# The weight conversion's stores begun by GpSimd instead of SyncE, and the post-softmax mix two places behind the pre-softmax mix

## The chip, the cores and the metric

One core of a Trainium2 chip. The metric is device time in microseconds (us) of one execution. Engines: PE (TensorE matmul; its weight loads are shown as PEld), DVE (VectorE), ACT (ScalarE), POOL (GpSimd), SP (SyncE, which here only begins DMAs).

## What is computed

Attention with heads mixed before and after the softmax, then a feed-forward layer. Cut to what matters:

```python
# batch 8, heads 12, seq 448, head_dim 64
scores = q @ k^T / 8                                   # per head
scores = einsum('bhij,hg->bgij', scores, w_pre)        # heads mixed
attn   = softmax over j
attn   = einsum('bhij,hg->bgij', attn, w_post)         # heads mixed again
x      = (attn @ v), rows = tokens (3584), columns = 12*64 = 768
h      = x @ w_in          # 768 x 2048, "in" weights
g      = h - tanh(h)
out    = g @ w_out         # 2048 x 768, "out" weights
```

## The kernel before, in words

The program has two stages. The first is attention (until about 845 us of the profile); the second is the feed-forward layer, whose products need each weight split into a rounded part and a remainder, and some sums and differences of weight quarters. This splitting, the **weight conversion**, is done during attention, on DVE, ACT and POOL, which have time left there.

**Attention.** Tokens of a batch come in blocks of 120 (the last has 88); a block's scores lie in SBUF as a tile `s`. Ten tokens by 12 heads make a group of 120 rows. A *place* handles two groups; there are 180 places (`NPL`), written out in Python in one loop over `p`, and every engine runs its instructions in exactly the order in which they are written (`in_order`). In place `p`:

1. SP begins the gathers `t<-s` (L907) of the groups that place `p+2` will need (`gather`, six tiles `t`), and then up to six waiting transfers of two lists, `queue` (loads of q, k, v and stores of x) and `slow` (the conversion's). A transfer is put in a list in one place and begun by SP in a later one (`issue`).
2. PE does the **premix** (`ps_p`, L918, 8 matmuls) of place `p`. Its two banks `ps_p` are the only ones, so it needs the exponents of place `p-1` to be finished.
3. `norm(p-1)`: DVE adds an epsilon to the sums and inverts them (`zs`, L938, L939), POOL multiplies them into the mixing weights (`wr`, L940).
4. `expo(p)`: DVE finds the row maxima (`mx`, L927, two), ACT the exponents (`e`, L929, two, four tiles).
5. PE does the jobs of the place: transposes of q and k (`ps_m` L840, L814), `scores` of a later block (`ps_q`, L874), and `values` (`ps_m`, L999), the product with v of an earlier block. The list `halved` gives each half of a block's scores ("s") and values ("v") an earliest and a latest place, and the loop behind it chooses.
6. PE does the **mix** of place `p-1` (`ps_o`, L957, 32 matmuls; one buffer of two banks), which needs `e` and `wr` of place `p-1`. ACT copies the result to `at` (L967, L974) at the start of the next place.

**The conversion.** `Convert.place` runs at the start of places 5 to 180. It takes a quad of four 128x128 weight pieces through the stages of the generator `narrow_quad`, one stage a place; 48 quads in all. Its DVE instructions (L81, L82, L90, L91, L94) stand ahead of the place's `zs` and `mx` in DVE's order, its POOL instructions (L84 to L131) ahead of the place's `wr`. Each quad is loaded as `cr` (two DMAs), and leaves by two stores of 512 KB, `co` and `ct`, to the tensors `wi`, `ss` (in) or `wo`, `ts` (out). The argument `dma` of `narrow_quad` puts these stores in the list `slow`, so SP begins them one place later or more.

POOL begins DMAs itself only in the feed-forward stage (`gs`, `go` and results, L647, L669, L670, L362, L519).

Of the kernel before, what the change touches and what calls it, by code (L numbers as in the profile page):

```python
# [10 lines left out]
F32 = mybir.dt.float32  # L11
# [10 lines left out]
def raw(ap):  # L22

    return ap.bitcast(F32)
# [10 lines left out]
class Convert:  # L35


    def __init__(self, nc, pool, dma, items, places):
        self.nc, self.pool, self.dma = nc, pool, dma
        self.todo, self.loads, self.active = list(items), [], []  # L40
        self.rate, self.due = len(self.todo) / places, 1.0

    def load(self):
# [6 lines left out]
    def place(self):  # L50
        for x in list(self.active):
            next(x[0], None)
            x[1] += 1
            if x[1] == 7:
                self.active.remove(x)
        self.due = min(self.due + self.rate, 1.3)
        if self.due >= 1.0 and len(self.active) < 2 and not [x for x in self.active if x[1] < 4] and self.loads and self.loads[0][1]():
            r, _, to = self.loads.pop(0)
            self.active.append([narrow_quad(self.nc, self.pool, self.dma, r, *to), 1])
            next(self.active[-1][0])  # L60
            self.due -= 1.0
        if self.todo and len(self.loads) < 2 and len(self.loads) + len([x for x in self.active if x[1] < 5]) < 3:
            self.load()

    def rest(self, between):
        while self.todo or self.loads or self.active:
            self.due = 1.0
            self.place()
            between()


def narrow_quad(nc, pool, dma, r, dst, sums, sums_dst):

    p = r.shape[0]
    hi, lo = r[:, :, :, 1], r[:, :, :, 0]
    u, w = hi, lo


    lim = 122879.9921875
    m = pool.tile([p, 4, 128], F32, name="cm", tag="cm", bufs=2)  # L80
    nc.vector.tensor_scalar(m, hi.bitcast(F32), lim, -lim, op0=ALU.min, op1=ALU.max)  # L81
    nc.vector.tensor_scalar(w, lo, 8, None, op0=ALU.logical_shift_right)  # L82
    yield
    nc.gpsimd.tensor_scalar(m, m, 2.0**-112, None, op0=ALU.mult)  # L84
    nc.scalar.mul(w.bitcast(F32), w, 2.0**-44)
    yield
    o = pool.tile([p, 4, 2, 128], F32R, name="co", tag="co", bufs=2)
    oh, ol = o[:, :, 0], o[:, :, 1]
    s = ol.bitcast(I32)
    nc.vector.tensor_scalar(s, hi, -(2**31), None, op0=ALU.bitwise_and)  # L90
    nc.vector.scalar_tensor_tensor(  # L91
        out=u, in0=m.bitcast(I32), scalar=3, in1=s, op0=ALU.logical_shift_left, op1=ALU.bitwise_or
    )
    nc.vector.tensor_scalar(s, u, -(2**23), None, op0=ALU.bitwise_and)  # L94
    yield
    nc.gpsimd.tensor_tensor(out=m, in0=w.bitcast(F32), in1=s.bitcast(F32), op=ALU.mult)
    nc.gpsimd.tensor_tensor(out=m, in0=m, in1=u.bitcast(F32), op=ALU.add)
    yield
    t = pool.tile([p, 4, 2, 128], F32, name="ct", tag="ct", bufs=2)
    nc.scalar.copy(oh, m)  # L100
    done = sums(nc, m, t[:, :, 1])
    yield
    nc.gpsimd.tensor_sub(ol, m, raw(oh))
    done()
    nc.gpsimd.tensor_copy(t[:, :, 0].bitcast(F32R), t[:, :, 1])
    dma(dst, raw(o).rearrange("p x t n -> p x (t n)"))
    yield
    nc.gpsimd.tensor_sub(t[:, :, 1].bitcast(F32R), t[:, :, 1], t[:, :, 0])
    dma(sums_dst, t.rearrange("p s t n -> p s (t n)"))


def sums_in(nc, m, t):
# [38 lines left out]
def kernel_body(  # L151
# [11 lines left out]
    nc = tc.nc  # L163
    B, H, S, D = q.shape
    P = 128
# [204 lines left out]
    class Results:  # L370
# [145 lines left out]
        def store(self, b, t, h, c):  # L516
            to = out[b * TB + t * TT : b * TB + (t + 1) * TT, h * N2 : (h + 1) * N2]
            eng = nc.gpsimd if self.n_gr < len(self.grs) else nc.sync
            eng.dma_start(to, c.rearrange("p c n -> p (c n)"))  # L519
# [216 lines left out]
    with ExitStack() as st:  # L736
# [184 lines left out]
        def expo(p, pss):  # L921
            zs = gp.tile([P, 3, 2], F32, name="zs", tag="zs")
            es = []
            for r, ps in enumerate(pss):

                mx = gp.tile([P, 1], F32, name="mx", tag="mx")
                nc.vector.tensor_reduce(out=mx, in_=ps, axis=AX.X, op=ALU.max, negate=True)  # L927
                e = gp.tile([P, S], F32, name="e", tag="e", bufs=4)
                nc.scalar.activation(e, ps, AF.Exp, bias=mx, scale=1.0, accum_out=zs[:, 0, r : r + 1])  # L929
                es.append(e)  # L930
            te[p] = [es, zs]
# [222 lines left out]
        for i in range(len(blocks)):  # L1154

            f0, f1, f2 = first[i : i + 3]
            if i + 1 < len(blocks):
                lo = max(0, (f0 - 1) // 2 - 1)
                hi = f1 // 2 - 3
                for x in range(0 if i else 1, 3):  # L1160
                    e = lo + 2 * x if lo + 4 <= hi else lo + (hi - lo) * x // 2
                    halved.append((e if i else x - 1, hi, "s", i + 1, x))
            for x in range(2):
                halved.append(((f1 - 1) // 2 + 2, f2 // 2 + 1 if f2 < NG else NPL + 7, "v", i, x))
        at_s, p, kind = {}, 0, None
        window = {i: (lo, hi) for lo, hi, k, i, _ in sorted(halved, reverse=True) if k == "s"}
        while halved:
# [84 lines left out]
            NPL - 1: [partial(load_w0, 1)],  # L1252
            NPL + 1: [block0.step],
        }
        mixed = None
        for p in range(NPL + 3):
            if mixed:
                mixed()
                mixed = None
            if 5 <= p < NPL + 1:  # L1260
                conv.place()
            place[0] += 1
            for t in (2 * p + 4, 2 * p + 5):
                if t < NG:
                    gather(t)
            issue(6)
            if p == NPL + 1:
                for f in start.pop(p):
                    f()
            if p < NPL:  # L1270
                ps = premix(p)
            if 1 <= p < NPL + 1:
                norm(p - 1)
            if p == NPL:
                for f in x0[1:]:
                    f()
            if p < NPL:
                expo(p, ps)
            if p > NPL:
                next(xq)  # L1280
                next(xq)
            for f, *a in todo[p]:
                f(*a)
            for f in sooner:
                f()
            sooner.clear()
            if 1 <= p < NPL + 1:
                mixed = mix(p - 1)
            for f in then + last:
                f()  # L1290
            then.clear()
            last.clear()
            if p == NPL - 3:
                conv.rest(now)
                early.close()
                open_early()
            if p == NPL - 1:
                early_ps.close()
                open_ps_h()
            for f in start.get(p, ()):  # L1300
                f()
            for _ in range(pieces.get(p, 0)):
                next(xl)
# [91 lines left out]
```

## Time and profile before

| | |
|---|---|
| three runs | 1707.81 us median (1704.64 to 1708.6) |
| the profiled execution | 1703.0 us, its span 1701.3 us |
| mean granted TensorE clock | 0.994 |
| busy in the span: PE, DVE, ACT, POOL | 1660.1, 1231.3, 1091.1, 585.5 us |
| DMAs begun by SP (queue q1) | 414.34 MB |
| DMAs begun by POOL (queue q0) | 57.68 MB |

The page lists, for each engine, how long it was busy; a view by stages gives the same for stretches of the span, with the granted clock of TensorE ("PEclk", 1.00 is full) and the busy share of the 16 DMA engines. "A <- B" in a list of waits means that A stood idle until B was done. In a timeline the columns are start, duration, engine, line and operation, and in brackets the idle time of that engine just before, with what ended it.

### The profile page before, as it was taken

How to read it: one execution, taken by the hardware profiler on the slowest of the kernel's cores; microseconds unless marked ns; L12 is line 12 of the kernel's file. 1: busy time of each engine (PE TensorE's matmuls, PEld its weight loads, DVE VectorE, ACT ScalarE, POOL GpSimd, SP SyncE). 2: the span in 40 equal slices, each digit the busy share in tenths (PEclk: the TensorE clock that was granted, in tenths of full speed). 3: DMA queues.
4: the chain of work that ended last, by engine and by line, in shares of the span. 5: the costliest groups of instructions: out<-in, count | busy, mean ns of one | idle time of the engine just before them, and what ended most of it. 6: DMA issues, size and time to landing. Idle time of an engine off the chain costs nothing.

```text
span 1701.3 us, 41215 instructions
## 1 busy us (share of the span) xinstructions
PE 1660.1 (98%) x16068; PEld 1379.8 (81%) x16068; DVE 1231.3 (72%) x2119; ACT 1091.1 (64%) x1920; POOL 585.5 (34%) x798
## 2 busy tenths in 40 slices
PE   8999999999999899999999999999999999999999
PEld 6777777777777677677788888888888888989999
DVE  5777777878777777675497899868778867778432
ACT  5777777777777677676586777556667456666331
POOL 1466667666666666662100111101001101011100
PEclk9999999999999999999999999999999999999999
DMA  8879889898987979856589899989999989988993
GB/s 183 218 228 257 255 246 276 247 270 259 256 253 231 269 234 257 254 182 208 190 269 340 273 331 318 346 295 335 318 334 362 368 272 327 326 311 327 404 413 132
DMA packets 322290, 475.09 MB, mean 279 GB/s; under 512 B 105264, under 2 KB 255280, under 8 KB 322096
## 3 DMA queue, kind: packets, MB, share of 16 engines
q1 hardware_dynamic: 305660, 414.34, 75.5%
q0 software_dynamic: 16128, 57.68, 8.7%
q8 instruction: 128, 2.10, 0.5%
q14 instruction: 66, 0.54, 0.1%
q10 hardware_dynamic: 308, 0.43, 0.1%
HBM read 274.73 MB, written 120.59 MB: 232 GB/s over the span
## 4 chain that ended last, share of the span: by engine, by line
PE 72%; DMA 7%; DVE 7%; ACT 4%; issue 4%; POOL 4%; SPq 1%; POOLq 0%; ACTq 0%; DVEq 0%
PE ps_o L957 11%; PE ps_h L291 8%; PE ps_h L292 7%; PE ps_h L294 7%; PE ps_m L999 6%; PE ps_p L918 6%; PE y L534 6%; PE y L532 6%; PE y L533 6%; PE ps_q L874 4%; DMA t<-s 2%; DMA gl<-gs 2%; ACT e L929 1%; DVE mx L927 1%; PE y L504 1%
## 5 line engine op out<-in xcount | busy, mean ns | idle before, releaser
L957 PEld LDWEIGHTS ps_o<-wr,e 60*112 60x112 f32 (+1 forms) x5760 | 303.3, 175 | 46.1 <-POOL wr L940 31.9
L957 PE MATMUL ps_o<-wr,e 60*112 60x60 f32 (+1 forms) x5760 | 314.5, 259 | 16.1 <-POOL wr L940 14.6
L929 ACT ACTIVATE e<-ps_p,mx 128x448 f32<-128x448 f32 x360 | 224.8, 631 | 117.2 <-DVE mx L927 82.8
L927 DVE TENSOR_REDUCE mx<-ps_p 128x1 f32<-128x448 f32 x360 | 206.5, 615 | 109.1 <-PE ps_p L918 108.5
L967 ACT COPY at<-ps_o 112x960 f32<-112x960 f32 x156 | 154.3, 989 | 103.4 <-PE ps_o L957 102.9
L918 PE MATMUL ps_p<-t,wpre 60*64 60x448 f32 (+1 forms) x1440 | 182.4, 570 | 6.7 <-DMA t<-s 6.6
L999 PEld LDWEIGHTS ps_m<-at,vr 112*64 112x64 f32 x3072 | 147.6, 137 | 23.0 <-issue 7.7
L999 PE MATMUL ps_m<-at,vr 112*64 112x120 f32 (+1 forms) x3072 | 161.4, 262 | 1.1 <-DMA vr<-in_v_dram 0.9
L532 PE MATMUL y<-w,gh 128*128 128x384 f32 x448 | 151.2, 338 | 2.1 <-DMA w<-wo 1.6
L940 POOL TENSOR_TENSOR wr<-wpost,zs 128x120 f32<-128x120 f32 x180 | 70.0, 389 | 237.6 <-DVE zs L939 199.0
L533 PE MATMUL y<-w,gh 128*128 128x384 f32 x448 | 150.5, 336 | 0.0
L534 PE MATMUL y<-w,gl 128*128 128x384 f32 x424 | 143.4, 338 | 3.0 <-DVE gl L450 3.0
L874 PEld LDWEIGHTS ps_q<-kk,qh 64*120 64x120 f32 (+1 forms) x768 | 59.1, 174 | 82.0 <-issue 45.1
L874 PE MATMUL ps_q<-kk,qh 64*120 64x448 f32 (+1 forms) x768 | 121.8, 394 | 0.9 <-ACT kk L825 0.4
L879 DVE COPY s<-ps_q 120x448 f32<-120x448 f32 (+1 forms) x192 | 112.2, 614 | 9.8 <-PE ps_q L874 8.0
L669 POOL DMA_DIRECT2D gs<-gb x24 | 17.2, 717 | 291.6 <-DVE gb L668 291.6
L307 ACT ACTIVATE u<-h 128x1024 f32<-128x1024 f32 x56 | 59.5, 1063 | 74.4 <-DVE h L716 70.5
L879 ACT COPY s<-ps_q 120x448 f32<-120x448 f32 (+1 forms) x192 | 94.9, 538 | 7.1 <-PE ps_q L874 6.7
L647 POOL DMA_DIRECT2D gs<-ga x24 | 17.2, 716 | 230.0 <-DVE ga L330 222.9
L532 PEld LDWEIGHTS y<-w,gh 128*128 128x128 f32 x448 | 84.2, 188 | 7.2 <-issue 3.5
L533 PEld LDWEIGHTS y<-w,gh 128*128 128x128 f32 x448 | 84.1, 188 | 3.4
L534 PEld LDWEIGHTS y<-w,gl 128*128 128x128 f32 x424 | 79.6, 188 | 4.6 <-DVE gl L450 4.6
(372 smaller groups left out, 3971.3 us busy)
## 6 DMA issues: line engine op xcount, KB each, us to landing
t<-s SPq DMA_DIRECT2D x342, 210.0 KB
wa<-ss SPq DMA_DIRECT2D x96, 384.0 KB
w<-wo SPq DMA_DIRECT2D x43, 768.0 KB
gl<-gs SPq DMA_DIRECT2D x62, 512.0 KB
wa<-wi SPq DMA_DIRECT2D x72, 384.0 KB
w<-ts SPq DMA_DIRECT2D x35, 768.0 KB
gs<-gs POOLq DMA_DIRECT2D x24, 768.0 KB, 9.2
cr<-in_moe_w_in_dram SPq DMA_DIRECT2D x48, 256.0 KB
```

The source lines that it names most:

```text
L291: nc.tensor.matmul(ph, w[:, c, 0], xh, start=start and c == 0, stop=False, skip_group_check=True)
L532: nc.tensor.matmul(y, gh[:, tok], wh, start=first, stop=False, skip_group_check=True)
L533: nc.tensor.matmul(y, gh[:, tok], wl, start=False, stop=False, skip_group_check=True)
L534: nc.tensor.matmul(y, gl[:, tok], wh, start=False, stop=last, skip_group_check=True)
L874: nc.tensor.matmul(ps[:n, :S], qx[a, hp, :], kx[a, hp % 2], start=(x == 0), stop=(x == 2))
L879: eng(sts[i][:n, 2 * hp + j, :], ps[:n, :S])
L918: nc.tensor.matmul(pss[r][halves[j], :], wpre[k, :], ts[j][k, :], start=True, stop=True)
L927: nc.vector.tensor_reduce(out=mx, in_=ps, axis=AX.X, op=ALU.max, negate=True)
L929: nc.scalar.activation(e, ps, AF.Exp, bias=mx, scale=1.0, accum_out=zs[:, 0, r : r + 1])
L957: nc.tensor.matmul(ps[:CP, j, c * GP : (c + 1) * GP].rearrange("p (h i) -> p h i", i=GI)[:, :, r * GH : (r + 1) * GH], e[k, c * CP : (c + ...
L967: nc.scalar.copy(ats[i0][:, :, :, at : at + 2 * GI].rearrange("p c h (j i) -> p j (c h) i", j=2), ps[:CP, :, : NC * GP].rearrange("p j (x ...
L999: nc.tensor.matmul(pv[j * D : (j + 1) * D, r, :n], vt[:, j, c, :], ats[i][:, c, 2 * hp + j, :n], start=(c == 0), stop=(c == NC - 1),)
```

## The change

Three things are edited. First, `narrow_quad` hands its stores to a list `done`, and a new method `Convert.stores`, called in each place just behind `norm(p-1)`, begins what is in it with `nc.gpsimd.dma_start`. Second, the mix of place `p-2` instead of `p-1` is written in place `p`, with the exponents in six tiles instead of four; in the last place (`NPL`) two mixes are left and are written one behind the other, with ACT's copy between them. The values of a block are allowed one place later. Third, the SBUF that is set aside for the DMAs that POOL begins is halved, 4096 to 2048 bytes.

```diff
-        self.todo, self.loads, self.active = list(items), [], []
+        self.todo, self.loads, self.active, self.done = list(items), [], [], []
...
-            self.active.append([narrow_quad(self.nc, self.pool, self.dma, r, *to), 1])
+            self.active.append([narrow_quad(self.nc, self.pool, lambda *x: self.done.append(x), r, *to), 1])
...
+    def stores(self):
+        for x in self.done:
+            self.nc.gpsimd.dma_start(*x)
+        self.done.clear()
...
-def narrow_quad(nc, pool, dma, r, dst, sums, sums_dst):
+def narrow_quad(nc, pool, store, r, dst, sums, sums_dst):
...
-    dma(dst, raw(o).rearrange("p x t n -> p x (t n)"))
+    store(dst, raw(o).rearrange("p x t n -> p x (t n)"))
...
-    dma(sums_dst, t.rearrange("p s t n -> p s (t n)"))
+    store(sums_dst, t.rearrange("p s t n -> p s (t n)"))
...
-                e = gp.tile([P, S], F32, name="e", tag="e", bufs=4)
+                e = gp.tile([P, S], F32, name="e", tag="e", bufs=6)
...
-                halved.append(((f1 - 1) // 2 + 2, f2 // 2 + 1 if f2 < NG else NPL + 7, "v", i, x))
+                halved.append(((f1 - 1) // 2 + 3, f2 // 2 + 2, "v", i, x) if f2 < NG else ((f1 - 1) // 2 + (3 if f1 < NG else 2), NPL + 7, "v", i, x))
...
         for p in range(NPL + 3):
-            if mixed:
-                mixed()
-                mixed = None
+            for f in mixed:
+                f()
+            mixed.clear()
...
             if 1 <= p < NPL + 1:
                 norm(p - 1)
+            conv.stores()
...
-            if 1 <= p < NPL + 1:
-                mixed = mix(p - 1)
+            if 2 <= p < NPL + 1:
+                mixed.append(mix(p - 2))
+            if p == NPL:
+                mixed.pop()()
+                mixed.append(mix(p - 1))
...
-    nc = _bacc.Bacc("TRN2", target_bir_lowering=False, num_devices=1, dynamic_dma_scratch_size=4096)
+    nc = _bacc.Bacc("TRN2", target_bir_lowering=False, num_devices=1, dynamic_dma_scratch_size=2048)
```

Line numbers behind the new method are 6 higher in the changed kernel (the mix is L963, the premix L924, `wr` L946, the values L1005).

How the order moves. On PE, from the premix of place 1 on, before:

```order
L918 MATMUL ps_p<-t,wpre 64x448 x4
L874 MATMUL ps_q<-kk,qh 120x448 x4
L874 MATMUL ps_q<-kk,ql 120x448 x2
L957 MATMUL ps_o<-wr,e 112x12x5 x16
L918 MATMUL ps_p<-t,wpre 64x448 x4
```

and with the change:

```order
L924 MATMUL ps_p<-t,wpre 64x448 x4
L880 MATMUL ps_q<-kk,qh 120x448 x4
L880 MATMUL ps_q<-kk,ql 120x448 x2
L924 MATMUL ps_p<-t,wpre 64x448 x4
L880 MATMUL ps_q<-kk,qh 120x448 x4
L880 MATMUL ps_q<-kk,ql 120x448 x2
L963 MATMUL ps_o<-wr,e 112x12x5 x16
```

Place 1 has no mix any more; the first mix stands behind the premix of place 2. (A row of the mix or the premix counts each matmul once, where the profile counts two passes.)

At the end of attention on PE, before (`ps_h` is the first product of the feed-forward layer):

```order
L957 MATMUL ps_o<-wr,e 112x12x5 x16
L918 MATMUL ps_p<-t,wpre 64x448 x4
L999 MATMUL ps_m<-at,vr 64x120 x24
L957 MATMUL ps_o<-wr,e 112x12x5 x16
L918 MATMUL ps_p<-t,wpre 64x448 x4
L957 MATMUL ps_o<-wr,e 112x12x5 x32
L291 MATMUL ps_h<-xh,w_13143 128x512
```

and with the change:

```order
L963 MATMUL ps_o<-wr,e 112x12x5 x16
L924 MATMUL ps_p<-t,wpre 64x448 x4
L1005 MATMUL ps_m<-at,vr 64x120 x24
L963 MATMUL ps_o<-wr,e 112x12x5 x16
L924 MATMUL ps_p<-t,wpre 64x448 x4
L1005 MATMUL ps_m<-at,vr 64x120 x24
L963 MATMUL ps_o<-wr,e 112x12x5 x48
L297 MATMUL ps_h<-xh,w_13097 128x512
```

Behind the last premix stood two mixes (x32); now a product of values and three mixes (x48) stand there.

On POOL, the second half of a quad's conversion, before:

```order
L940 TENSOR_TENSOR wr<-wpost,zs 128x2x60
L103 TENSOR_TENSOR co<-cm,co 128x4x128
L105 CAST ct<-ct 128x4x128
L940 TENSOR_TENSOR wr<-wpost,zs 128x2x60
L108 TENSOR_TENSOR ct<-ct 128x4x128
L96 TENSOR_TENSOR cm<-cr,co 128x512
L97 TENSOR_TENSOR cm<-cm,cr 128x512
L940 TENSOR_TENSOR wr<-wpost,zs 128x2x60
```

and with the change:

```order
L946 TENSOR_TENSOR wr<-wpost,zs 128x2x60
L109 TENSOR_TENSOR co<-cm,co 128x4x128
L111 CAST ct<-ct 128x4x128
L946 TENSOR_TENSOR wr<-wpost,zs 128x2x60
L67 DMA wi_65<-co 512x1x256
L114 TENSOR_TENSOR ct<-ct 128x4x128
L102 TENSOR_TENSOR cm<-cr,co 128x512
L103 TENSOR_TENSOR cm<-cm,cr 128x512
L946 TENSOR_TENSOR wr<-wpost,zs 128x2x60
L67 DMA ss_77<-ct 512x1x256
```

Each store stands just behind a `wr`; 96 such DMAs are on POOL, and SP's order has 96 fewer.

More of the change, by code (lines that the diff above doesn't have):

```diff
@@ L68, in rest @@
             self.place()
+            self.stores()
             between()
-def narrow_quad(nc, pool, dma, r, dst, sums, sums_dst):
+def narrow_quad(nc, pool, store, r, dst, sums, sums_dst):
     p = r.shape[0]
@@ L1254, in kernel_body @@
         }
-        mixed = None
+        mixed = []
         for p in range(NPL + 3):
-            if mixed:
-                mixed()
-                mixed = None
+            for f in mixed:
+                f()
+            mixed.clear()
             if 5 <= p < NPL + 1:
```

## Prediction

> **What bounds the kernel now.** I read the page's busy times first, then the stages, then what PE waited for in attention.
>
> ```profile
> PE 1660.1 (98%) x16068; PEld 1379.8 (81%) x16068; DVE 1231.3 (72%) x2119; ACT 1091.1 (64%) x1920; POOL 585.5 (34%) x798
> ```
>
> ```profile
> core 0: us, PE busy (x) PEld busy (x) DVE busy (x) ACT busy (x) POOL busy (x), PEclk, DMA share, GB/s
> 60.00:760.00 700.00, 680.61 (x9930) 521.58 (x9925) 523.69 (x1315) 500.82 (x1146) 470.53 (x597) 0.99 0.83 248
> 760.00:870.00 110.00, 107.38 (x1434) 84.19 (x1431) 63.49 (x146) 70.67 (x146) 20.80 (x37) 0.98 0.65 211
> 870.00:1701.00 831.00, 817.16 (x4116) 732.74 (x4114) 610.51 (x576) 484.84 (x553) 82.85 (x128) 1.00 0.89 321
> ```
>
> PE is the bound in every stage. In the 700 us in which the conversion runs, PE is idle for only 19.4 us, and POOL for 229.5. The change adds or removes no work on PE, so all that it can win is PE's idle time in attention, some 20 us, and what the clock loses there. The feed-forward stage I take as it is: what POOL begins there it begins as before, and POOL is busy for a tenth of that stage. What PE waited for, from 0 to 760 us:
>
> ```profile
> engine line waited for: us in total, times, longest us
> PE ps_o L957 <- POOL wr L940: 13.4, 16, 1.7
> PE ps_p L918 <- DMA t<-s: 6.6, 8, 1.6
> ```
>
> Two kinds of wait: the mix for its weights `wr`, and the premix for its gathers. The change is aimed at both.
>
> **Part 1: the mix two places behind.** One of the longest waits for `wr`, around 103 us, and one late in the stage:
>
> ```profile
> 102.33 0.43 DVE L94 TENSOR_SCALAR co<-cr 128x512 int32<-128x512 int32 x1
> 103.00 1.14 DVE L927 TENSOR_REDUCE mx<-ps_p 128x1 f32<-128x448 f32 x2
> 103.22 0.39 POOL L940 TENSOR_TENSOR wr<-wpost,zs 128x120 f32<-128x120 f32 x1 [3.54 <-DVE zs L939]
> 103.66 1.78 PE L957 MATMUL ps_o<-wr,e 60*112 60x60 f32 x32 [1.56 <-POOL wr L940]
> 104.32 0.62 ACT L929 ACTIVATE e<-ps_p,mx 128x448 f32<-128x448 f32 x1
> 105.38 0.98 PE L918 MATMUL ps_p<-t,wpre 60*64 60x448 f32 x8
> ...
> 564.46 1.78 PE L957 MATMUL ps_o<-wr,e 60*112 60x60 f32 x32 [1.27 <-POOL wr L940]
> 565.11 0.62 ACT L929 ACTIVATE e<-ps_p,mx 128x448 f32<-128x448 f32 x1
> 566.18 0.61 PE L918 MATMUL ps_p<-t,wpre 60*64 60x448 f32 x4
> ```
>
> Here POOL was not late (3.54 us idle). DVE was: the conversion's L90, L91 and L94 stood ahead of `zs`. With the mix a place later, `wr` has about one more place (some 4 us: 700 us for about 170 places), more than the longest wait of 1.7, so all 13.4 us of these waits go. But the same DVE instructions also stand ahead of `mx`, and what is late next is the exponent: the second one ends at 104.94, and the next premix, which needs its bank, starts at 105.38. Had PE not waited for 1.56 us, the premix could have moved up by 0.44 only. I went through all the waits for `wr` in this way, place by place. Six (at 103.7, 153.3, 210.3, 358.3, 554.9 and 564.5 us) have less room than their wait: 6.67 us of waits have 2.58 us of room, so 4.1 us come back as waits for exponents. In the others, the longest at 593.5 and 719.6 us among them, the room exceeds the wait. Gain: 13.4 - 4.1 = 9.3 us, with ends 4 (the room halves, since DVE and ACT don't come earlier as PE does) and 13.4.
>
> **The clock.** Three of these waits are followed by a lower clock:
>
> ```profile
> 590.00:595.00 5.00, 3.27 (x50) 2.32 (x43) 4.37 (x7) 3.45 (x9) 4.11 (x4) 1.00 1.04 232
> 595.00:600.00 5.00, 5.00 (x50) 3.26 (x48) 2.24 (x7) 3.17 (x8) 3.08 (x4) 0.66 0.92 311
> 695.00:700.00 5.00, 5.00 (x57) 3.26 (x52) 3.46 (x7) 3.93 (x10) 2.25 (x3) 0.75 0.95 251
> 720.00:725.00 5.00, 5.00 (x48) 3.24 (x48) 2.88 (x7) 2.25 (x6) 4.11 (x4) 0.66 0.99 252
> ...
> 593.53 0.70 PE L957 MATMUL ps_o<-wr,e 60*112 60x60 f32 x10 [1.73 <-POOL wr L940]
> 719.56 0.70 PE L957 MATMUL ps_o<-wr,e 60*112 60x60 f32 x9 [1.62 <-POOL wr L940]
> ```
>
> A window at 0.66 has lost 0.34 of 5 us, 1.7 us of PE's time; three such dips (the second, just before and behind 695 us, is cut by the window's edge) cost 5.1 us. Each begins within 2 us of the end of a wait for `wr` of 1.0 to 1.7 us; waits as long at 103.7 and 210 us had no dip, so a wait only makes one likely. I take two of three as gone: 3.4 us, ends 0 and 5.1. [...]
>
> **Part 2: the stores begun by POOL.** What a store costs POOL is not in the trace; DMAs that POOL begins in the feed-forward stage are, with 1 piece a partition (L519, L362), 2 (L669) and 3 (L670). A store of the conversion has 4:
>
> ```profile
> L519 POOL DMA_DIRECT2D out_dram<-c x48: 540/540/580, 1099.7 to 1665.6; - x48
> L669 POOL DMA_DIRECT2D gs<-gb x24: 707/718/732, 956.6 to 1573.8; - x24
> L670 POOL DMA_DIRECT2D gs<-gs x24: 750/760/778, 957.3 to 1574.5; - x24
> ...
> L105 POOL CAST ct<-ct 128x512 fp32r<-128x512 f32 x46 | 29.8, 649 | 63.1 <-ACT ct L131 51.3 <-DVE zs L939 11.8
> L103 POOL TENSOR_TENSOR co<-cm,co 128x512 fp32r<-128x512 f32 x47 | 60.3, 1282 | 23.2 <-ACT co L100 23.1
> ```
>
> The third piece cost 42 ns, the second 178. I take 0.80 us (0.76 + 0.04), nearest to the last step, with ends 0.54 and 0.94. 96 stores are 77 us, which lie in POOL's 229.5 us of idle time; 74 of these are waits of POOL for ACT that remain, which leaves 155 us, or 1.65 us a store. Behind a store in POOL's order stand the conversion's next steps and then the next place's `wr`, which now has a place to spare: no cost on PE. If that cover is gone, DVE's L91 and ACT's L100, which need the conversion's POOL steps, hold up `mx` and the exponents behind them.
>
> SP loses 96 issues. Seven of its gathers were late in the steady part (6.6 us less the first, 1.65 us at the start of the program, is 5.0), mostly behind single issues that held SP for 5 to 6 us:
>
> ```profile
> 25.21 1.77 PE L918 MATMUL ps_p<-t,wpre 60*64 60x448 f32 x8 [1.65 <-DMA t<-s]
> 158.61 6.68 SPq L766 DMA_DIRECT2D cr<-in_moe_w_in_dram  x2
> 161.35 0.98 PE L918 MATMUL ps_p<-t,wpre 60*64 60x448 f32 x8 [0.85 <-DMA t<-s]
> L766 SPq DMA_DIRECT2D ts<-ct x24: 577/651/6125, 431.4 to 781.5; - x24
> ```
>
> Such an issue was a load as well as a store, and total DMA traffic stays, so I give only 1.5 of the 5.0 us: ends 5.0, and -3.0, because `values` now come up to a place later while the loads of v that overwrite their input stay where they were; SP can stand at such a load with gathers queued behind it, three to four times at under 1 us (as the row above). The smaller DMA space costs nothing that a row shows: POOL's 57.68 MB in the feed-forward stage are spread over 720 us.
>
> **Part 3: the ends.** At the start place 1 loses its mix, but the next premix waits for the exponent; at the end PE has that mix more, and three mixes in a row share one buffer:
>
> ```profile
> 30.71 1.73 PE L957 MATMUL ps_o<-wr,e 60*112 60x60 f32 x32
> 31.41 0.62 ACT L929 ACTIVATE e<-ps_p,mx 128x448 f32<-128x448 f32 x1
> 32.37 0.98 PE L918 MATMUL ps_p<-t,wpre 60*64 60x448 f32 x8
> ...
> 839.95 1.78 PE L957 MATMUL ps_o<-wr,e 60*112 60x60 f32 x32 [0.26 <-ACT at L967]
> 841.77 0.97 ACT L967 COPY at<-ps_o 112x960 f32<-112x960 f32 x1
> 842.89 2.01 PE L957 MATMUL ps_o<-wr,e 60*112 60x60 f32 x32 [1.16 <-POOL wr L940]
> ```
>
> The exponent ends at 32.03, the premix began at 32.37: 0.3 us are won there, and 1.66 (30.71 to 32.37) paid at the end. Two of three mixes there wait for a copy of 0.97 and some 0.13 around it: 2.2 us, where now 0.26 + 1.16 = 1.4 are waited. Cost: 1.66 - 0.3 + 0.8 = 2.1 us, ends 0.5 and 3.
>
> **The sum** against the profiled execution: -9.3 - 3.4 - 1.5 + 2.1 = -12.1 us, 1703.0 to 1690.9. The profiled execution is 4.8 us below the median of the three runs, 1707.81, and 1.6 below their fastest. The same 12.1 us off the median give 1695.7; I predict 1696.
>
> **Rivals.** (a) *The exponents take the wait over.* PE ahead meets `ps_p` unfinished in many places: DVE is busy for 75% of the stage (523.69 of 700) and ACT for 72%, and a premix often starts a few tenths behind the last exponent. For it speaks the 103 us row; against it, that PE's waits are few and most have room. Only 4 us of part 1 and no dip remain won: 1707.8 - 4 - 1.5 + 2.1 = 1704.4.
>
> (b) *POOL becomes the bound* (slower). It decides where a store costs POOL more than 1.65 us. At 2.0 us, POOL would lack 0.35 x 94 = 33 us, the steps behind would drag DVE and ACT with them, and the time would be 1696 + 33 = 1729. For it: an SP issue of the same store has taken 6.1 us; against it, no POOL issue has exceeded 0.8.
>
> ```profile
> L90 DVE TENSOR_SCALAR co<-cr x48: 407/418/1023, 59.2 to 761.5; 128x512 int32<-128x512 int32 x48
> L84 POOL TENSOR_SCALAR cm<-cm x48: 1484/1490/1505, 53.1 to 758.1; 128x512 f32<-128x512 f32 x48
> ```
>
> These rows show who gives way now: L90 takes 407 ns or up to 1023, L84 on POOL always the same. A store that gave way to one such DVE instruction would cost 0.8 + 0.42 = 1.22 us, still under 1.65. [...]
>
> (c) *Gathers get later*: nothing of their 5.0 us is won, SP's stands at the loads of v cost their 3.0, and a dip follows one: 1695.7 + 1.5 + 3.0 + 1.7 = 1701.9. For it: the DMA engines were busy throughout where gathers were late (share 1.04 from 590 to 595); against it: SP has fewer DMAs ahead of each gather.
>
> (d) *All waits go*, gathers too, and the exponents follow PE: -13.4 - 5.1 - 5.0 + 2.1 = -21.4, or 1686.
>
> **How the numbers follow.** A measurement of this kernel can tell about 0.3%, 5 us, from no change. Chances: the forecast 0.62 (1690 to 1702), (a) 0.18, (b) 0.07, (c) 0.08, (d) 0.05. Faster by over 0.3% (under 1702.7): the forecast, (d), half of (c) and a third of (a): 0.77. Slower by over 0.3% (above 1712.9): (b), 0.07. The same: 0.16. The range leaves out (b) and the far side of (c) and (d): 1686 to 1707.
>
> **What would show it.** In the changed kernel's waits, no mix (L963) waits for `wr` but at the end of attention; premix waits for exponents, about 4 us in total, stand in their place; the dips at 595, 694 and 721 us are mostly gone; L67 on POOL takes about 0.8 us, and POOL is busy for about 545 us from 60 to 760. The prediction is wrong if premixes wait for exponents for over 9 us, if L67 exceeds 1.65 us, or if the time moves in the feed-forward stage.

## The result: slower, with all of it in attention

The changed kernel takes 1759.43 us (median; 1752.41 to 1770.68), the kernel before 1708.2 beside it: 1.030 of before, 95% interval 1.026 to 1.034. The prediction was 1696. The profiled execution of the changed kernel took 1758.4 us with a span of 1756.7 and a mean granted clock of 0.978.

The first line of the profile's page after, and the two stages (attention, then feed-forward; the boundary is the first `ps_h`), first before, then after, columns as in the prediction:

```profile
PE 1697.9 (97%) x16068; PEld 1406.0 (80%) x16068; DVE 1281.4 (73%) x2119; ACT 1090.4 (62%) x1920; POOL 663.6 (38%) x894
```

```profile
0.00:844.80 844.80, 817.75 (x11772) 626.35 (x11772) 603.90 (x1530) 592.22 (x1353) 499.94 (x667) 0.99 0.81 239
844.80:1701.30 856.50, 842.34 (x4298) 753.43 (x4296) 627.42 (x590) 498.90 (x569) 85.58 (x131) 1.00 0.89 319
```

```profile
0.00:901.10 901.10, 857.42 (x11773) 654.56 (x11773) 653.92 (x1530) 591.70 (x1353) 580.71 (x766) 0.96 0.75 225
901.10:1756.70 855.60, 840.47 (x4298) 751.41 (x4296) 627.46 (x589) 498.68 (x567) 82.86 (x128) 1.00 0.89 318
```

Attention is 56.3 us longer, feed-forward 0.9 shorter. In attention PE's idle time rises from 27.05 to 43.68 us (+16.6) and its busy time by 39.7, though its work is the same. In the trace's record of the granted clock, TensorE is at half of full speed (half clock) in 5 windows that begin in attention (17.1 us) before, and in 16 (78.5 us) after. Within attention PE was busy for 14.1 and 71.7 us of these, and half of the difference, 28.8 us, is lost. The other 11 us are mostly premixes drawn out, which means that more time lies between a premix's first matmul and its last (below). PE's waits, after:

```profile
engine line waited for: us in total, times, longest us
PE ps_p L924 <- ACT e L935: 24.2, 20, 2.6
PE ps_p L924 <- DMA t<-s: 12.3, 9, 3.5
```

The mix's waits for `wr` are gone, as forecast. But the premix now waits 24.2 us for exponents where 4.1 were forecast, and for its gathers 12.3 where 6.6 stood. One such wait, from where it starts (timeline of the changed kernel):

```profile
599.63 0.86 POOL L67 DMA_DIRECT2D wo<-co  x1 [0.16 <-POOL wr L946]
600.44 2.90 DVE L87 TENSOR_SCALAR cm<-cr 128x512 f32<-128x512 f32 x1
600.51 1.29 POOL L114 TENSOR_TENSOR ct<-ct 128x512 fp32r<-128x512 f32 x1
601.74 1.31 POOL L102 TENSOR_TENSOR cm<-cr,co 128x512 f32<-128x512 f32 x1
603.13 1.36 POOL L103 TENSOR_TENSOR cm<-cm,cr 128x512 f32<-128x512 f32 x1
603.27 1.50 DVE L88 TENSOR_SCALAR cr<-cr 128x512 int32<-128x512 int32 x1
605.01 1.14 DVE L933 TENSOR_REDUCE mx<-ps_p 128x1 f32<-128x448 f32 x2
605.71 0.63 ACT L935 ACTIVATE e<-ps_p,mx 128x448 f32<-128x448 f32 x1 [3.51 <-DVE mx L933]
606.49 2.38 PE L924 MATMUL ps_p<-t,wpre 60*64 60x448 f32 x8 [2.23 <-ACT e L935]
```

The store on POOL takes 0.86 us, as forecast. Behind it L114 and L102 follow each other without a gap, and DVE's clamp L87, which takes 0.41 us alone, stands through both: 2.90 us. The shift L88 stands through L103. So `mx` comes late, the exponent, the premix; and behind the wait the clock halves (PEclk, the column after POOL, is 0.66 from 605 to 610):

```profile
600.00:605.00 5.00, 3.92 (x46) 2.58 (x46) 4.96 (x6) 2.20 (x6) 4.39 (x4) 1.00 1.10 326
605.00:610.00 5.00, 3.52 (x14) 1.58 (x16) 3.13 (x9) 4.13 (x10) 4.45 (x7) 0.66 0.86 275
```

These two DVE instructions, summed over the 48 quads, before and after:

```profile
L82 DVE TENSOR_SCALAR cr<-cr 128x512 int32<-128x512 int32 x48 | 37.9, 790 | 0.0
L81 DVE TENSOR_SCALAR cm<-cr 128x512 f32<-128x512 f32 x48 | 37.4, 779 | 2.3 <-DMA cr<-in_moe_w_in_dram 2.3
```

```profile
L87 DVE TENSOR_SCALAR cm<-cr 128x512 f32<-128x512 f32 x48 | 65.3, 1360 | 0.0
L88 DVE TENSOR_SCALAR cr<-cr 128x512 int32<-128x512 int32 x48 | 54.3, 1132 | 0.0
```

75.3 us became 119.6. I call them "the clamp and the shift" from here on.

### The profile page after: what moved, and what is told of

Its sections match the earlier page's. It is cut to its first block, busy times and chain, and to the rows that moved or that the text cites. A ratio compares the mean times of both kernels' runs of the same rounds, so it can differ in the third digit from the quotient of the medians.

```text
span 1756.7 us, 41149 instructions
## 1 busy us (share of the span) xinstructions
PE 1697.9 (97%) x16068; PEld 1406.0 (80%) x16068; DVE 1281.4 (73%) x2119; ACT 1090.4 (62%) x1920; POOL 663.6 (38%) x894
## 4 chain that ended last, share of the span: by engine, by line
PE 71%; DVE 13%; DMA 7%; ACT 5%; issue 3%; SPq 0%; POOL 0%; ACTq 0%; DVEq 0%; POOLq 0%
PE ps_o L963 10%; PE ps_p L924 8%; PE ps_h L297 7%; PE ps_h L298 7%; PE ps_h L300 7%; PE ps_m L1005 7%; PE y L540 6%; PE y L538 6%; PE y L539 5%; PE ps_q L880 5%; DMA t<-s 4%; DVE cm L87 2%; ACT e L935 2%; DVE mx L933 2%; DMA gl<-gs 2%
## 5 line engine op out<-in xcount | busy, mean ns | idle before, releaser
L963 PEld LDWEIGHTS ps_o<-wr,e 60*112 60x112 f32 (+1 forms) x5760 | 312.3, 177 | 21.9 <-issue 6.5
L963 PE MATMUL ps_o<-wr,e 60*112 60x60 f32 (+1 forms) x5760 | 316.6, 260 | 3.1 <-POOL xl L286 1.7
L924 PE MATMUL ps_p<-t,wpre 60*64 60x448 f32 (+1 forms) x1440 | 207.6, 588 | 36.8 <-ACT e L935 24.2
L1005 PEld LDWEIGHTS ps_m<-at,vr 112*64 112x64 f32 x3072 | 152.6, 140 | 18.7 <-issue 9.3
L1005 PE MATMUL ps_m<-at,vr 112*64 112x120 f32 (+1 forms) x3072 | 166.3, 266 | 0.0
L946 POOL TENSOR_TENSOR wr<-wpost,zs 128x120 f32<-128x120 f32 x180 | 70.6, 392 | 219.4 <-DVE zs L945 158.1
L880 PE MATMUL ps_q<-kk,qh 64*120 64x448 f32 (+1 forms) x768 | 129.8, 412 | 1.5 <-DVE kk L832 0.5
L924 PEld LDWEIGHTS ps_p<-t,wpre 64*64 64x64 f32 (+1 forms) x1440 | 47.3, 135 | 63.9 <-ACT e L935 40.9
```

Of the source, the lines that this page charges most:

```text
L880: nc.tensor.matmul(ps[:n, :S], qx[a, hp, :], kx[a, hp % 2], start=(x == 0), stop=(x == 2))
L924: nc.tensor.matmul(pss[r][halves[j], :], wpre[k, :], ts[j][k, :], start=True, stop=True)
L963: nc.tensor.matmul(ps[:CP, j, c * GP : (c + 1) * GP].rearrange("p (h i) -> p h i", i=GI)[:, :, r * GH : (r + 1) * GH], e[k, c * CP : (c + ...
L1005: nc.tensor.matmul(pv[j * D : (j + 1) * D, r, :n], vt[:, j, c, :], ats[i][:, c, 2 * hp + j, :n], start=(c == 0), stop=(c == NC - 1),)
```

## The experiments

Medians in us; each ratio is to runs of the kernel before (1708.2 to 1709.9) on the same chip. Waits are PE's in attention, from each run's profiled execution.

| run | what it is | time | ratio, 95% | waits for `e`; gathers | clamp + shift |
|---|---|---|---|---|---|
| before | | 1708 | 1 | 0 (`wr` 14.6); 6.6 | 75.3 |
| after | the change | 1759.4 | 1.030 (1.026 to 1.034) | 24.2; 12.3 | 119.6 |
| e1 | stores alone | 1755.3 | 1.024 (1.019 to 1.030) | 0 (`wr` 36.2); 3.6 | 114.5 |
| e2 | mix alone | 1725.5 | 1.009 (1.005 to 1.012) | 4.8; 17.5 | 78.3 |
| e3 | after, stores ahead of `wr` | 1738.7 | 1.015 (1.008 to 1.022) | 8.7; 21.7 | 93.9 |
| e4 | e2 + one memset | 1725.7 | 1.008 (1.005 to 1.011) | 7.0; 15.0 | 83.5 |
| e5 | after, conversion behind exponents | 1809.9 | 1.060 (1.053 to 1.067) | 7.8; 10.7 | 162.8 |
| e6 | before, conversion behind exponents | 1729.5 | 1.011 (1.005 to 1.017) | 0 (`wr` 9.9); 10.5 | 99.1 |
| e7 | e2, loads of v apart | 1707.4 | 0.998 (0.995 to 1.001) | 5.6; 7.7 | 80.0 |
| e8 | e2 + two memsets | 1727.7 | 1.010 (1.004 to 1.016) | 10.7; 13.7 | 85.9 |
| e9 | after, stores between | 1732.1 | 1.015 (1.011 to 1.019) | 12.1; 16.0 | 96.8 |
| e10 | after, loads of v apart | 1748.5 | 1.023 (1.020 to 1.027) | 25.4; 7.1 | 122.5 |
| e11 | e9 and e7 together | 1721.7 | 1.007 (1.005 to 1.010) | 13.8; 9.1 | 100.6 |
| e12 | before, loads of v apart | 1747.7 | 1.024 (1.020 to 1.027) | 0 (`wr` 14.9, v 24.2); 1.6 | 76.1 |
| e13 | e2 + POOL load, 32 bytes | 1741.8 | 1.021 (1.017 to 1.025) | 20.5; 12.4 | 109.9 |
| e14 | e2 + POOL load, 512 pieces | 1760.8 | 1.031 (1.028 to 1.033) | 25.2; 10.7 | 120.8 |
| e15 | e7 + two memsets between | 1710.7 | 1.001 (0.998 to 1.003) | 10.4; 5.1 | 80.9 |
| e16 | e7, written otherwise | 1706.7 | 0.999 (0.997 to 1.001) | 4.8; 12.1 | 79.4 |
| e17 | e7, half maxima | 1700.3 | 0.995 (0.992 to 0.997) | 3.3; 10.1 | 80.8 |
| e18 | before, half maxima | 1707.1 | 0.999 (0.998 to 1.001) | 0 (`wr` 12.8); 5.9 | 76.9 |

**Which part does it: e1 and e2.** Each takes one half of the change alone.

```diff
 e1: the kernel before, with
+            self.nc.gpsimd.dma_start(*x)      (Convert.stores, behind norm(p - 1))
 e2: the changed kernel, with
-            self.active.append([narrow_quad(self.nc, self.pool, lambda *x: self.done.append(x), r, *to), 1])
+            self.active.append([narrow_quad(self.nc, self.pool, self.dma, r, *to), 1])
```

> The kernel before with the stores alone moved to POOL, behind norm(p-1); mix of place p-1, four exponent tiles, 4096 bytes. Theory A (a store's 0.8 us between wr and the conversion's next POOL steps makes DVE's two plain instructions of a new quad, L81 and L82, arrive while POOL runs two steps without a gap, and wait for both): L81 and L82 together rise from 1.57 us a quad to about 2.4, and since wr still has no place to spare, 1740 to 1765 us. Rival B (the mix two places behind is what costs: PE runs ahead and DVE and ACT fall behind): L81 and L82 as before, 1700 to 1710 us. Rival C (a DMA begun by POOL costs by itself, through its descriptors or its queue): 1740 to 1765 us.

> The changed kernel with the stores back on SP, in the list slow: the mix two places behind, six exponent tiles and 2048 bytes alone. Theory A: DVE as before (L81 and L82 together about 1.6 us a quad), no waits for wr, 1690 to 1702 us. Rival B: premixes wait for exponents for over 20 us, 1735 to 1765 us. Rival C: 1690 to 1702 us.

Both halves lose. The stores alone cost 47 us, and there the wait that grows is the mix's for `wr`. The smaller DMA space is no part of that: e1 has the old 4096 bytes, and its clamp and shift take 114.5 us. The mix alone costs 17, a time that lies between all of its forecasts. Its waits for `e` are as the prediction had them (4.8 us for 4.1); what grew is the waits for gathers:

```profile
PE ps_p L924 <- DMA t<-s: 17.5, 10, 3.5
PE ps_p L924 <- ACT e L935: 4.8, 7, 1.1
```

They come about once a batch. The same premix in e2 and in the kernel before (place 32), and the clock behind it (e2, then before):

```profile
166.14 1.77 PE L924 MATMUL ps_p<-t,wpre 60*64 60x448 f32 x8 [3.52 <-DMA t<-s]
```

```profile
166.21 0.98 PE L918 MATMUL ps_p<-t,wpre 60*64 60x448 f32 x8 [0.93 <-DMA t<-s]
```

```profile
165.00:170.00 5.00, 3.86 (x26) 2.30 (x28) 1.16 (x2) 1.29 (x5) 1.67 (x4) 0.50 1.00 251
```

```profile
165.00:170.00 5.00, 4.07 (x64) 3.16 (x64) 1.51 (x4) 3.18 (x8) 2.89 (x6) 1.00 0.97 247
```

The gather lands at the same time in both (the premix starts at 166.14 and 166.21 us), and the DMA engines are full there (share 1.00 and 0.97 from 165 to 170). PE, which was ahead in e2, waits for it in one piece, 3.52 us, and then runs at 0.50 where before it ran at 1.00.

**Where the store stands: e3, e4, e5, e6.** e4 is e2 with one memset (128x384, 0.42 us) on POOL where a store would stand.

```diff
 e3
+            conv.stores()
...
             if 1 <= p < NPL + 1:
                 norm(p - 1)
-            conv.stores()
 e4
+                self.nc.gpsimd.memset(self.fill, 0.0)
 e5 and e6
-            if 5 <= p < NPL + 1:
-                conv.place()
...
             if p < NPL:
                 expo(p, ps)
+            if 5 <= p < NPL + 1:
+                conv.place()
```

> The changed kernel with one move: the stores stand on POOL behind the conversion's steps and ahead of norm's wr, instead of behind it. The same 96 stores, the same mix. Theory A: POOL waits there for zs anyway, the steps behind wr begin on time, L87 and L88 (L81 and L82 before) are back near 1.6 us a quad, 1690 to 1710 us. Rival B: as the changed kernel, 1750 to 1765 us. Rival C: as the changed kernel, 1750 to 1765 us.

> The stores on SP as before, the mix two places behind, and where the changed kernel has a store on POOL one memset of 128x384 that nothing reads stands instead (about 0.4 us, half a store's time). It adds work and leaves nothing out. Theory A: time on POOL at this place is what matters, so L87 and L88 rise, less than with a store: 1715 to 1750 us. Rival B: as the mix alone, 1735 to 1765 us. Rival C: no DMA of POOL, so nothing: 1690 to 1702 us.

> The changed kernel with one move: the conversion's step of a place is written behind the place's exponents instead of ahead of its gathers, so that VectorE's two maxima (mx) stand ahead of the conversion's VectorE instructions of the place, and the stores stay on GpSimd. Theory A (a store on GpSimd pushes the conversion's GpSimd steps together, VectorE's clamp and shift wait for them, and mx stands behind on VectorE): premix's waits for e fall from 24.4 us to under 8, the time at half clock from 78.5 us to under 50, and the time from 1759 to about 1722-1732, the level of the mix two places behind by itself (1725). Theory C (a store begun by GpSimd costs by itself, whatever stands behind): the waits for e shrink little and the time stays over 1745.

> The kernel before with the same move alone (the conversion's step of a place behind the place's exponents; stores on SyncE, mix one place behind). Theory A: the mix's waits for wr (15.2 us) come from the conversion's work ahead of zs and mx on VectorE and ahead of wr on GpSimd, so they fall under 6 us, the dips of the clock behind them go too, and the time falls to about 1690-1700. Rival: the waits for wr come from wr's own GpSimd queue (the steps of the place before reach past it) and stay, and the time is 1705-1712.

e3 gets back 21 us, and lies between its forecasts. e4 takes the time of e2 (1725.7 for 1725.5); it is inside its forecast of 1715 to 1750 only because e2 itself stands there. No forecast of the time of e5 or e6 holds. e5 does what it should to the waits for `e` (7.8), and is slower by 50: the clamp and the shift now stand ahead of the copies of scores, and PE waits there. So writing them elsewhere moves the damage; e6 loses 21 us, with no store on POOL. The waits of e5:

```profile
PE ps_q L880 <- DVE zs L944: 13.8, 12, 2.5
PE ps_p L924 <- DMA t<-s: 10.7, 6, 5.4
PE ps_m L846 <- DVE s L885: 10.3, 4, 3.0
```

**Time on POOL, or a transfer on POOL: e8, e13, e14.** All are e2 (stores on SP) with something else on POOL where the changed kernel begins a store: two memsets; a load of 32 bytes that nothing reads; the same in 512 pieces.

```diff
+            self.nc.gpsimd.memset(self.fill, 0.0)             (e8, twice: 128x384)
+            self.nc.gpsimd.dma_start(few, self.few)           (e13: 1 piece; e14: 128x4 pieces of 32 bytes)
```

> The mix two places behind with stores on SyncE, and where the changed kernel begins a store on GpSimd two memsets of 128x384 there instead (0.42 us each, 0.84 together, as long as a store's 0.73-0.86). Theory A (it is the time on GpSimd ahead of the conversion's steps): as the changed kernel, 1745-1760, with waits for e of 15 us or more and a sum of the two big VectorE steps of 105 us or more. Theory C (it is the transfer that GpSimd begins, not the time): as with one memset, 1720-1730, with waits for e under 10 us and the sum under 95 us.

> The mix two places behind with all stores on SyncE, and where the changed kernel begins a store on GpSimd, GpSimd begins a load of 32 bytes there instead that nothing reads. Theory D1 (a transfer begun by GpSimd directly ahead of two GpSimd instructions is enough to keep VectorE out between them): clamps and shifts of 105 us or more in 48 quads where the mix two behind has 78, premix's waits for e over 14 us, 1740-1760. Theory D2 (it needs the store's many pieces or its leaving SyncE): as the memsets there, under 90 us and 1722-1732.

> The same with a load of 512 pieces of 32 bytes (four in each of 128 partitions, as many pieces as a store of the changed kernel has). Theory D1: as with the one piece, or more by the longer time on GpSimd (1745-1765). Theory D3 (it is the writing of many pieces' descriptors): 105 us or more and 1740-1760 here, but not with the one piece. Theory D4 (neither: it is the stores' leaving SyncE): under 90 us and 1722-1735 in both.

This settles which of the two it is. Two memsets of 0.43 us each change next to nothing against e2 (1727.7 for 1725.5, with intervals that overlap). One transfer of 32 bytes (585 ns on POOL) costs 16 us, and one with a store's number of pieces (807 ns) costs 35 and gives the changed kernel's time, waits and sums, though every store is still on SP. Both are as forecast by D1. D3 fails with the first of them, and the writing of descriptors that it names is seen in no trace. Why the second costs twice the first is seen only in part: its clamp and shift take 11 us more, and its half clock is 75.1 us against 41.0. The POOL groups of e8, e13 and e14 (count, busy, mean ns):

```profile
L73 POOL MEMSET fill<- 128x384 f32 x192 | 82.7, 430 | 5.5
```

```profile
L72 POOL DMA_DIRECT2D few<-in_q_dram x96 | 56.2, 585 | 4.5 <-ACT e L940 1.5 <-issue 0.2
```

```profile
L72 POOL DMA_DIRECT2D few<-in_q_dram x96 | 77.4, 807 | 9.6 <-issue 9.1 <-DMA t<-s 0.3
```

What differs can be seen in one place at the same distance: the clamp starts 0.6 to 0.7 us into the subtraction, with a store ahead of that (changed kernel) and with a memset ahead (e8).

```profile
135.96 0.77 POOL L67 DMA_DIRECT2D wi<-co  x1 [0.15 <-POOL wr L946]
136.70 1.34 POOL L114 TENSOR_TENSOR ct<-ct 128x512 fp32r<-128x512 f32 x1
137.31 2.29 DVE L87 TENSOR_SCALAR cm<-cr 128x512 f32<-128x512 f32 x1
137.94 1.36 POOL L102 TENSOR_TENSOR cm<-cr,co 128x512 f32<-128x512 f32 x1
139.38 1.38 POOL L103 TENSOR_TENSOR cm<-cm,cr 128x512 f32<-128x512 f32 x1
```

```profile
135.76 0.42 POOL L73 MEMSET fill<- 128x384 f32 x1
136.13 1.28 POOL L120 TENSOR_TENSOR ct<-ct 128x512 fp32r<-128x512 f32 x1
136.84 0.86 DVE L93 TENSOR_SCALAR cm<-cr 128x512 f32<-128x512 f32 x1
137.37 1.49 POOL L108 TENSOR_TENSOR cm<-cr,co 128x512 f32<-128x512 f32 x1
138.94 1.36 POOL L109 TENSOR_TENSOR cm<-cm,cr 128x512 f32<-128x512 f32 x1
```

With the memset DVE gets in between (it ends 0.29 us behind the subtraction, and the multiplication gives way: 1.49 for 1.36). With the store it gets in only behind the multiplication.

Counted over the traces: take a clamp that starts while this subtraction runs, outlasts it, and has the multiplication following without a gap. It ended 1.53 to 1.56 us behind the subtraction in 61 of 61 cases where a POOL-begun transfer stood directly ahead (after, e1, e5, e10, e13, e14), and 0.28 to 0.41 us behind it in 58 of 58 where the kernel has none there (before, e2, e4, e6, e7, e8). A clamp or shift that met the transfer itself, ahead of the same two, stood through both in 35 of 36 cases (until 2.84 to 2.87 us behind the transfer). But it isn't so for every pair: in the same six kernels a clamp that met the multiplication directly behind a transfer, with the subtraction L103 next, ended 0.29 to 0.30 us behind the multiplication in 32 of 32. Nor is it transfers alone: in e3, with `wr` between the store and the subtraction, 6 of 8 stood through both, and in e15 a memset that followed the subtraction was stood through in 8 of 8. What decides this in POOL or DVE is not shown.

**Stores between the two: e9.**

```diff
+        ready, self.done = self.done, []                  (the stores that were ready when the place began)
         for x in list(self.active):
             next(x[0], None)
+            while ready:
+                self.nc.gpsimd.dma_start(*ready.pop(0))
...
-            conv.stores()                                 (behind norm(p - 1))
```

> The changed kernel with the stores, still begun by GpSimd, moved from behind wr to the place between the older quad's last subtraction (ct) and the younger quad's multiplication (cm), which stood next to each other behind the store. Theory D (in the trace, VectorE's clamp and shift that meet the running subtraction end 0.28 us behind it where no store stands directly ahead of it, and 1.54 us behind it, after the multiplication too, where one does; a gap of a store's length there lets VectorE in): the clamp and shift of the 48 quads fall from 119.6 us to under 90, premix's waits for e from 24.4 to under 12, the time from 1759 to 1722-1735. Theory C (any store on GpSimd costs this): over 1745, waits for e over 18 us.

With the store between the subtraction and the multiplication no clamp or shift stands through both any more, and 27 of the 51 us come back, as forecast. The clamp and the shift take 96.8 us, though, where under 90 was forecast: 14 of them met the store itself and stood on through the multiplication, until 1.62 to 1.65 us behind the store.

**The loads of v: e7, e10, e11, e12.**

```diff
-                    at_place(p0 + 4 + hq, load_v, b, hq)
+                    at_place(p0 + 4 + 2 * hq, load_v, b, hq)
```

> The mix two places behind with stores on SyncE, and the three loads of the values v of a batch asked for two places apart instead of one. Theory B1 (the mix two behind loses its gain where the loads of a batch fill the DMA engines and premix meets its gather: waits for gathers 17.5 us in seven places, each with a window of half clock): the long waits for gathers shrink to under 9 us, the time at half clock from 47.8 to about 30, the time from 1725 to 1705-1715. Rival B2 (the load of k and of the weights fill the engines anyway): waits for gathers over 14 us and 1720-1730.

> The changed kernel with the three loads of v of a batch two places apart. If the gathers' part and the stores' part of the loss are separate, the 18 us that this spacing gave with the stores on SyncE come off here too: 1737-1745, waits for gathers from 12.4 to under 8 us, those for e stay at 20-25. If they are one loss (the clock's), the time falls by less than 8 us: over 1751.

> Both edits: the stores between the subtraction and the multiplication, and the loads of v two places apart. If both parts of the loss are named rightly: 1700-1715, with under 9 us of waits for gathers and under 12 for e. If a part is left unnamed: over 1720.

> The kernel before with the loads of v two places apart, nothing else. If the crowded transfers cost only a PE that runs ahead: 1705-1710, no change beyond 0.3%. If the gathers' waits of before (6.7 us) and the mix's wait for v go too: 1695-1704. Slower than 1712 if the values then wait for their v.

With the three loads two places apart, the mix alone gains 18 us (e7). In the changed kernel the same edit gives 11 (e10), between its two forecasts, so the two parts of the loss overlap a little. The kernel before cannot use it (e12): its values come a place earlier and wait for their v.

```profile
PE ps_m L999 <- DMA vr<-in_v_dram: 24.2, 8, 5.5
```

e11 missed its forecast by 7 us: even with DVE let in, stores on POOL cost 14 us over e7.

e15 and e16 go on from e7:

```diff
 e15, between the older quad's subtraction and the younger's multiplication
+            while ready:
+                ready.pop(0)
+                for _ in range(2):
+                    self.nc.gpsimd.memset(self.fill, 0.0)
...
 e16, at the last place
+            if p == NPL:
+                mix(p - 2)()
             for f, *a in todo[p]:
                 f(*a)
...
```

> The mix two places behind with the loads of v apart and the stores on SyncE, and two memsets (0.84 us) on GpSimd where the stores stood in the run with both edits (1721.7): between the older quad's subtraction and the younger's multiplication. If what was left of the stores' cost there (14 us over the 1707.4 without them) is GpSimd's time: 1717-1726, waits for e over 11 us. If it is the transfers that GpSimd begins: 1705-1712, waits for e under 9 us.

Memsets of the same length there cost 3 us, so most of the 14 is again the transfers and not POOL's time. The two traces show one place where they differ: in e11 15 clamps or shifts that met the store stood on through the multiplication (until 1.63 to 1.64 us behind the store), and in e15 14 that met the second memset ended 0.28 us behind it. The clamp and the shift take 100.6 us in e11 and 80.9 in e15. Whether that is all of the difference is not shown.

> The mix two places behind with the loads of v apart and the stores on SyncE, and at the last place the mix of the place before last written ahead of that place's scores and values, so that its copy out of the accumulator runs beside them. At the end of the attention the waits for that copy (two of 1.17 us) and the 10.2 us at half clock behind them should go down to one wait and 3.4 us: 3-5 us less, 1702-1705, and 0.994-0.998 of before. If the exponents' waits that show only as a drawn-out premix (192.6 us busy against 182.4) eat it: 1706-1709.

The last place turned out to have no scores or values, so e16 issues the same instructions in the same order as e7 and serves as its repeat: 1706.7 and 1707.4. Its profile also tells how far one profile can be trusted: waits for gathers 12.1 and 7.7 us, half clock 30.7 and 17.1, in two executions of one program.

**Where the mix's gain went: e17, e18.** In e7 the waits for `wr` (14.6 us in all of attention) are gone, and only 5.6 us for `e`, and 3.0 for copies of scores, stand in their place; yet the time is that of before. The premix's own group, before, e7 and e17 (the same 1440 passes; busy us, mean ns):

```profile
L918 PE MATMUL ps_p<-t,wpre 60*64 60x448 f32 (+1 forms) x1440 | 182.4, 570 | 6.7 <-DMA t<-s 6.6
```

```profile
L924 PE MATMUL ps_p<-t,wpre 60*64 60x448 f32 (+1 forms) x1440 | 192.6, 563 | 17.4 <-DMA t<-s 7.7 <-ACT e L935 5.6 <-ACT s L885 3.0
```

```profile
L924 PE MATMUL ps_p<-t,wpre 60*64 60x448 f32 (+1 forms) x1440 | 187.2, 564 | 14.8 <-DMA t<-s 10.1 <-ACT e L935 3.3 <-ACT at L973 1.1
```

The four matmuls of a premix run beside each other: in the kernel before the eight passes of the one at 32.37 us, of 535 to 587 ns each, lie within 0.98 us. The first needs one of the two banks, freed by the first exponent, the second the other. In e7 25 of the 180 premixes start in part, over 0.3 us ahead of the rest (before: 5). One of them starts at 32.39 us in that profile, and the others of its matmuls 0.62 us later, behind the second exponent (which ends at 32.87); PE counts as busy meanwhile (1.59 us for this premix). The premixes are drawn out by 10.2 us in all, on top of the 5.6 that show as waits. e17 and e18 let exponents come earlier, with maxima over half of the columns (another shift of the softmax, which can be too small for other inputs):

```diff
-                nc.vector.tensor_reduce(out=mx, in_=ps, axis=AX.X, op=ALU.max, negate=True)
+                nc.vector.tensor_reduce(out=mx, in_=ps[:, : S // 2], axis=AX.X, op=ALU.max, negate=True)
```

> The mix two places behind with the loads of v apart and the stores on SyncE, and the maxima (mx) taken over the first half of the columns only (the softmax's shift is then another number). Each of the two VectorE instructions ahead of the exponents gets some 0.25 us shorter. Theory E (what the mix two behind gains on wr it loses on exponents, most of it as premixes drawn out, which no wait shows): premix's busy time falls from 192.6 us to 183-188, its waits for e from 5.6 to under 3, and the time from 1707 to 1690-1699, at least 5 us under the kernel before with the same half maxima. Rival (the drawn-out premix costs nothing, the gain went elsewhere): over 1700 and within 4 us of the other run.

> The kernel before with the same half maxima. VectorE has some 90 us less to do, wr comes no earlier than zs lets it, so the mix's waits for wr (15.2 us) fall by a few us at most: theory E 1700-1707. Rival: VectorE's load as such set the pace, and this run gains as much as the other: under 1699.

The kernel before gains nothing from it (0.999), the mix two behind does: 1700.3, 6.7 us under e18, with the premix's busy time at 187.2. In e17 13 premixes start in part. So exponents are what the mix two behind runs into. The size was a little under the forecast (1700.3 for 1690 to 1699). e17 is also the one version that beats both kernels, by 0.5% and 3.4%.

## Why the prediction was wrong, step by step

**Part 2, "no cost on PE".** This step failed, and it is the largest: 47 us alone (e1), 34 on top of the mix (after against e2). The store's price was right (0.73 to 0.86 us for the forecast 0.80; L67's means for its four targets are 730, 730, 765 and 855 ns, its longest 0.92 us), and POOL had the room, 581 us busy of 901. The argument looked for the cost in POOL's time, where e8 shows it isn't. I had the row that tells who gives way (DVE's L90 407 to 1023 ns, POOL's L84 1484 to 1505) and used it only for what a store might suffer; the store changed how long DVE gives way (75.3 to 119.6 us for the clamp and the shift), ahead of `mx`. The instructions that it named as held up, L91 and L100, need POOL's results; those that were held up, the clamp and the shift, read only the loaded `cr`. By the prediction's own sign, premixes waiting for exponents for over 9 us, it is wrong: they wait 24.2. Rival (b) had the right sign at a chance of 0.07, and a wrong mechanism and point of decision (1.65 us a store).

**Part 1, the mix's waits.** That all waits for `wr` go was right, and so was 4.1 us of waits for exponents (4.8 in e2). What failed is taking PE's waits for the whole price: premixes drawn out cost 10 us more (e7), and nothing was won. Rival (a), exponents take the wait over, was right for this part. In the changed kernel the stores raise these waits to 24.2 us.

**The gathers, -1.5 us with an end of +3.0.** The sign failed: +5.7 us in the changed kernel, +10.9 in e2, beyond the end. Rival (c) named the loads of v and a dip behind, and e7 shows that it was the right suspect; the row that gave its size (waits of under 1 us) was measured with PE behind, and a PE that runs ahead meets the whole lateness of the gather (3.52 us for 0.93 at 166 us).

**The clock, -3.4 us.** Right that waits of 1 us and more bring half clock: in the changed kernel it begins during the wait or within 2.5 us behind it in 15 of 17. Wrong in sign, since new waits came: 28.8 us lost. Half clock begins behind a wait of 2.23 us (606.49), and in the 3.4 us (the length of the shortest of the windows) ahead of each of the 16, PE was idle for 0.8 to 2.2 us in all. The dip of 595 us did not go: e2 has one at 591.2, behind a gather.

**The ends, +2.1 us.** In e7 the last two mixes wait 1.17 and 1.16 us for a copy, 2.3 against 1.4 before, as worked out; but half clock lasts 10.2 us behind the first where it was 3.4. Under-sized by some 3 us.

**Feed-forward unchanged** was right: 855.6 us for 856.5.

## What to carry to other kernels

Before work is put on an engine because it is idle, ask which other engine gives way to it, and whether what is held up there stands ahead of something that the bound engine needs: here 96 transfers of 32 bytes, 0.6 us each on an idle GpSimd, cost 16 us through VectorE. A wait removed on the bound engine is won only if its next input comes early enough (e7 lost the mix's 14.6 us of waits for `wr` and won no time; e17, with earlier exponents, took 1700.3); count the groups of matmuls that start in part, and not only its idle time, and expect a PE that gets ahead to meet the transfers' schedule, in one long wait that also costs the clock (3.52 us and a granted clock of 0.50 behind it in e2). Spread the transfers that crowd a batch's boundary before pulling the engine ahead (18 us in e7).

## What the runs showed of the hardware that I had not expected

- Directly behind a transfer that GpSimd begins, VectorE's clamp stood through a subtraction and the multiplication that follows it without a gap (61 of 61; up to 3.33 us for a clamp of 0.41, where it had met the transfer itself); with none ahead it got in after the subtraction (58 of 58). A load of 32 bytes is enough (e13: clamp and shift 109.9 us for e2's 78.3). With the multiplication first and a subtraction next it got in after the first, behind a transfer too (32 of 32).
- Waits of PE of 1.0 to 3.5 us are often followed by half clock for 3.4 us or more: 15 of 17 in the changed kernel, 9 of 12 in e2, 4 of 7 before. In e2 there are 9 windows and 47.8 us at half clock for 28.3 us of idle time in attention.
- Where the DMA engines are full, gathers that SP issued from 155.32 to 158.50 us for the premix at 166.14 (e2; DMA share 1.05, 0.88 and 1.00 in the three stretches of 5 us from 155 on) are still late: PE waits 3.52 us for them.
